# A convolution and GLU kernel: the GLU products as two 64-row tiles that change banks half way

## The chip, the cores and the metric

The kernel runs on one core of a Trainium2 chip. The metric is the device time of one execution in microseconds; two runs gave 587.36 and 587.61, median 587.49.

## The reference

A is a long convolution (S4D) over 2048 positions and 512 channels, B a bilinear GLU, and a gate per position mixes the two:

```python
g = sigmoid((x * gate_w).sum(-1, keepdims=True))
K = 2.0 * einsum("dn,dnl->dl", C, exp((A * dt)[:, :, None] * pos)).real
a = irfft(rfft(u_t, 2 * L) * rfft(K, 2 * L), 2 * L)[:, :, :L]   # transposed back, + u * D_skip
b = einsum("bsf,fd->bsd", (x @ w_gate) * (x @ w_up), w_down)    # F = 1792, D = 512
return g * a + (1 - g) * b
```

## The kernel before, in words

All GLU products are done in f32r, TensorE's rounded 32-bit form. For accuracy each operand is split into a rounded value (`hi`) and a remainder (`lo`), and each product of a 128-row block is three matmuls: lo·hi, hi·lo and hi·hi (`THREE`). The convolution (tiles named k) runs in plain float32, partly with small tiles of the array.

The GLU takes the 1792 hidden channels as 14 blocks `f` of 128, in four groups of 3, 3, 4 and 4 (`GROUPS`), and the 2048 positions in four chunks `ci` of 512. `glu()` (line 690) goes through the 16 pairs of group and chunk. For each `f` of the group, `hidden(f)` (line 596) computes gate and up: four contraction blocks `kt`, three matmuls each, into the PSUM bank `pg`, then the same into `pu`; each matmul has 128 columns of weights and 512 positions. That is 56 calls. Then a chain of four operations makes `h`: ScalarE copies `pg`, VectorE multiplies by `pu`, ScalarE rounds to `hh`, VectorE takes the remainder `hl`. Only the very first step (`f == 0` of the first chunk) goes by `kt` first and needs each part of the weights as it lands.

`down` (line 623) multiplies the group's `h` by the down weights, for the four 128-row blocks `r` of the chunk in two halves (0, 1) and (2, 3). Each block sums over the group's `f` in one bank `y`. For blocks 0 and 1 the products of the group's last `f` come last for both blocks (`late`), so that the chain to its `hl` has time. `evacuate` (line 634) scales a bank by 1 - g on ScalarE into `acc`, from where it is written or added to the output in DRAM; in the last group and chunk the sums stay on the chip, and blocks 2 and 3 are read by VectorE straight from PSUM in `ends` (line 655).

PSUM has eight banks. Line 401 gives the convolution four (`ps_k`) and the GLU four: `pg` and `pu` one each (`ps_g`) and `y` two in turn (`ps_y`).

The order of all work is set by a planner, the class `Work` (line 197). Each piece of work is a task with an engine, a duration, the tiles that it reads and writes, and a rank; `run` (line 301) lays the tasks out in time, each engine one after the other, picking what can start first and then the lower rank. `ready` (line 252) is when a task may follow another. The instructions are then issued in that order, and `InOrder` (line 116) holds every engine's order as it was laid out. So a changed task moves the order of everything after it. All instructions are issued through `InOrder`, which is why the profile shows one line, L124, for all. A GLU product is a task of 0.681 us (three matmuls).

A task may name parts of a tile, `(tile, part)`, and then waits only for work on the same part.

Of the kernel before, what the change touches and what calls it, by code (L numbers as in the profile page):

```python
# [18 lines left out]
P = 128  # L19
# [122 lines left out]
class Tile:  # L142


    def __init__(self, work, pool, tag, shape, dtype, bufs, loose):
        self.pool, self.tag, self.shape, self.dtype, self.bufs, self.loose = pool, tag, shape, dtype, bufs, loose
        self.writers, self.readers = [], []
# [13 lines left out]
        return self.ap  # L161


class Task:
    def __init__(self, n, engine, us, fn, rank, after, dma):
        self.n, self.engine, self.us, self.fn, self.rank, self.after, self.dma = n, engine, us, fn, rank, after, dma
        self.deps, self.tiles, self.start, self.end, self.rows, self.many = set(), [], None, None, (), 0


class Bus:  # L170
# [26 lines left out]
class Work:  # L197
# [8 lines left out]

    LAG = {"pe": 0.06, "sp": 0.3, "pool": 0.3}
    PE_LAG = 0.17

    OVERLAP = {"act": 0.09, "dve": 0.08}  # L210

# [89 lines left out]
    def run(self):  # L301
# [10 lines left out]
        while any(left.values()):  # L312
# [40 lines left out]
            rows.update((r, t.end) for r in t.rows)  # L353
            for tile in t.tiles:
                if tile.made is None:
                    tile.made = start
                    tile.had.append(tile)
            order.append(t)
        for t in order:
# [5 lines left out]
def gated_mix_kernel(  # L365
# [211 lines left out]

    THREE = ((1, 0), (0, 1), (0, 0))

    def product(pg, which, w, x, kt, after, first):  # L580
        base = which * D + kt * P
        part = ("k", kt) if first else which

        three = THREE[::-1] if first else THREE

        def fn():
            for n, (a, b) in enumerate(three):
# [4 lines left out]
        add("pe", 0.681, fn, r=[(w[0], part), (w[1], part), x], w=[pg], rank=2, after=after)  # L592

    steps = []

    def hidden(f):

        pg = [new("ps_g", n, [P, D]) for n in ("pg", "pu")]
        x = dict(xs)
        after = T_STEP * len(steps) - 5.0  # L600
        steps.append(f)
        pairs = [(which, kt) for which in range(2) for kt in range(KT)]
        if f == 0:

            pairs.sort(key=lambda p: p[1])
# [14 lines left out]
        )  # L620
        return hh, hl

    def down(y, r, h, w, first, last):
        def fn():
            for n, (a, b) in enumerate(THREE):
                pe.matmul(
                    y.t, h[a].t[:, r * P : (r + 1) * P], w[b].t, start=first and n == 0, stop=last and n == 2
                )

        add("pe", 0.681, fn, r=[*h, *w], w=[y], rank=2)  # L630

    ending = []

# [56 lines left out]
    def glu():  # L690
# [10 lines left out]
        for n, (gi, ci) in enumerate(order):  # L701
            fs = GROUPS[gi]
            if ci != old:
                if gi == 0 and ci <= 2:
                    ahead(ci)
                for kt in range(KT):
                    tokens(gi, ci, kt)
            old = ci
            hs = {f: hidden(f) for f in fs}
            ends = n % 4 == 3 and gi + 1 < len(GROUPS)  # L710
            if ends:
                weights(GROUPS[gi + 1])

            for rr in ((0, 1), (2, 3)):
                ys = {r: new("ps_y", "y", [P, D], bufs=2) for r in rr}
                late = fs[-1:] if rr[0] == 0 else []
                for r in rr:
                    for f in fs:
                        if f not in late:
                            down(ys[r], r, hs[f], wd[f], f == fs[0], f == fs[-1])  # L720
                    if not late:
                        evacuate(gi, ci, r, ys[r])
                if late:
                    for r in rr:
                        down(ys[r], r, hs[fs[-1]], wd[fs[-1]], False, True)
                        evacuate(gi, ci, r, ys[r])
            if ends:
                down_weights(GROUPS[gi + 1])

# [760 lines left out]
```

## Time and profile before

| | |
|---|---|
| median of two runs | 587.49 us |
| span of the profiled execution (first to last instruction) | 586.6 us |
| granted TensorE clock, mean | 1.000 |
| last matmul's start | 582.46 us |
| DMA, mean over the span | 232 GB/s |

The profiled execution's own time is 0.9 us over its span. In the profile PE is TensorE's matmuls and PEld its weight loads; DVE is VectorE, ACT ScalarE, POOL GpSimd, SP the engine that issues most DMAs. A row of the timeline has the start, the duration, the engine, the operation, the tile written and the tiles read, the array tile used (rows by columns), the shape, and how many were merged (x2); the bracket is the engine's idle time before it and what released it. Rows of groups have the total busy time and the mean of one in ns, then the idle time before them. Rows of waits have the total in us, the number and the longest. In the row of a stage each engine has its busy time and its number of instructions, in the order PE, PEld, DVE, ACT, POOL, then the granted clock, the DMA share and GB/s. A matmul's duration is modelled and covers its whole way through the array, so the next one starts before it ends.

### The profile page before, as it was taken

The numbers are of one execution on the slowest core, as the hardware profiler recorded it, in microseconds if no ns is written. First come the engines' busy times: TensorE is split into PE (matmuls) and PEld (weight loads), VectorE is DVE, ScalarE is ACT, GpSimd is POOL, SyncE is SP. The second block draws the span as 40 slices with busy tenths as digits, with TensorE's granted clock in tenths as the row PEclk, the third lists the DMA queues.
The fourth block names the chain that finished last, engine by engine and source line by source line (L and its number), as shares of the span: only waits on it lengthen the run. The fifth ranks groups of instructions, "written<-read, shape, count | busy, mean of one in ns | idle before, by whom it ended". The sixth has DMA issues, their size and how long they took to land.

```text
span 586.6 us, 14827 instructions
## 1 busy us (share of the span) xinstructions
PE 576.4 (98%) x5996; PEld 433.9 (74%) x5996; DVE 511.3 (87%) x812; ACT 399.0 (68%) x891; POOL 113.4 (19%) x159
## 2 busy tenths in 40 slices
PE   8999999999989999999999999999999999999997
PEld 5777777877876777887777778777878787677775
DVE  6998999999999999999799999995999982367664
ACT  5468888898578589876968764899696523443351
POOL 0002222311102231310412200421321104011011
PEclk9999999999999999999999999999999999999999
DMA  8999969997647698998697859899958349899976
GB/s 276 383 369 357 374 241 319 289 257 212 125 154 181 194 272 205 228 245 297 135 257 249 183 180 304 158 187 276 221 136 212 65 143 230 290 270 253 283 159 125
DMA packets 71687, 136.28 MB, mean 232 GB/s; under 512 B 6852, under 2 KB 35780, under 8 KB 69188
## 3 DMA queue, kind: packets, MB, share of 16 engines
q1 hardware_dynamic: 47668, 87.10, 43.0%
q0 software_dynamic: 23392, 47.98, 39.5%
q8 instruction: 47, 0.77, 0.6%
q10 hardware_dynamic: 560, 0.26, 0.2%
q14 instruction: 20, 0.16, 0.1%
HBM read 80.27 MB, written 55.05 MB: 231 GB/s over the span
## 4 chain that ended last, share of the span: by engine, by line
PE 83%; DVE 6%; ACT 4%; DMA 4%; issue 1%; SPq 0%; DVEq 0%; ACTq 0%
PE pg L124 23%; PE pu L124 23%; PE y L124 22%; PE k L124 16%; DVE v L124 1%; DMA pb<-par_d 1%; DMA xs_d<-xs 1%; DVE x L124 1%; DMA y<-in_xT 1%; DMA xs<-xs_d 1%; ACT acc L124 1%; DVE t L124 1%; ACT ev L124 1%; ACT xs L124 1%; ACT e L124 1%
## 5 line engine op out<-in xcount | busy, mean ns | idle before, releaser
L124 PE MATMUL pg<-xs,whi 128*128 128x512 f32 x448 | 138.9, 391 | 1.0 <-DVE xs L124 0.6
L124 PE MATMUL pu<-xs,whi 128*128 128x512 f32 x448 | 138.3, 390 | 0.0
L124 PEld LDWEIGHTS pg<-xs,whi 128*128 128x128 f32 x448 | 84.2, 188 | 20.2 <-ACT whi L124 2.0
L124 PEld LDWEIGHTS pu<-xs,whi 128*128 128x128 f32 x448 | 84.2, 188 | 16.9
L124 PE MATMUL y<-dhi,hl 128*128 128x512 f32 x224 | 90.3, 403 | 2.9 <-DVE hl L124 2.4
L124 PE MATMUL pu<-xs,wlo 128*128 128x512 f32 x224 | 90.1, 402 | 0.0
L124 PE MATMUL pg<-xs,wlo 128*128 128x512 f32 x224 | 89.4, 399 | 0.4 <-ACT h L124 0.4
L124 PE MATMUL y<-dlo,hh 128*128 128x512 f32 x224 | 87.5, 391 | 0.0
L124 PE MATMUL y<-dhi,hh 128*128 128x512 f32 x224 | 87.3, 390 | 0.0
L124 POOL DMA_DIRECT2D out<-acc x44 | 40.2, 968 | 180.4 <-ACT acc L124 173.0
L124 ACT COPY ev<-k 128x512 f32<-128x512 f32 x112 | 58.8, 596 | 14.5 <-PE k L124 14.4
L124 ACT CAST hh<-h 128x512 fp32r<-128x512 f32 x56 | 34.6, 618 | 45.7 <-DVE h L124 45.5
L124 PEld LDWEIGHTS y<-dhi,hl 128*128 128x128 f32 x224 | 42.0, 187 | 24.4 <-issue 8.1
L124 DVE TENSOR_TENSOR h<-pu,h 128x512 f32<-128x512 f32 x56 | 38.5, 688 | 23.6 <-PE pu L124 23.0
L124 PEld LDWEIGHTS pu<-xs,wlo 128*128 128x128 f32 x224 | 42.0, 187 | 20.0 <-issue 10.7
L124 ACT ACTIVATE acc<-y,ngate 128x512 f32<-128x512 f32 x62 | 41.7, 685 | 21.9 <-PE y L124 18.9
L124 PEld LDWEIGHTS pg<-xs,wlo 128*128 128x128 f32 x224 | 42.1, 188 | 18.4 <-issue 6.9
L124 ACT COPY h<-pg 128x512 f32<-128x512 f32 x56 | 32.9, 587 | 28.3 <-PE pg L124 22.0
L124 PEld LDWEIGHTS y<-dhi,hh 128*128 128x128 f32 x224 | 42.1, 188 | 9.1
L124 PEld LDWEIGHTS y<-dlo,hh 128*128 128x128 f32 x224 | 42.1, 188 | 8.2 <-DVE dlo L124 0.3
L124 DVE TENSOR_TENSOR hl<-h,hh 128x512 fp32r<-128x512 f32 x56 | 38.4, 686 | 3.0 <-ACT hh L124 2.7
L124 PEld LDWEIGHTS k<-v,x 128*32 128x32 f32 x2048 | 30.6, 109 | 6.4 <-issue 4.7
(130 smaller groups left out, 965.4 us busy)
## 6 DMA issues: line engine op xcount, KB each, us to landing
xs<-xs_d SPq DMA_DIRECT2D x36, 512.0 KB, 5.8
out<-acc POOLq DMA_DIRECT2D x44, 256.0 KB, 5.9
raw<-in_wts SPq DMA_DIRECT2D x33, 256.0 KB, 5.6
xs_d<-xs SPq DMA_DIRECT2D x16, 512.0 KB, 6.6
su_d<-ev POOLq DMA_DIRECT2D x32, 256.0 KB, 6.3
y_d<-ts SPq DMA_DIRECT2D x28, 256.0 KB, 4.9
in<-su_d POOLq DMA_DIRECT2D x12, 512.0 KB, 5.9
sk_d<-ev SPq DMA_DIRECT2D x6, 1024.0 KB, 5.4
```

The lines of the kernel that those rows point to most:

```text
L124: got = getattr(self.engine, name)(*args, **kw)
```

## The change

A new helper, `paired`, takes over all GLU products except the first gate/up step. It works for two PSUM banks at a time: `pg` and `pu` in `hidden`, or the two row blocks' `y` in `down`. Every 128-row contraction block is cut into two 64-row halves, each with its own 64-row tile of the array (`tile_position` 0 and 64). In the first half of a call tile 0 (upper rows) works for bank 0 and tile 1 (lower rows) for bank 1; then TensorE is drained, and in the second half tile 0 works for bank 1 and tile 1 for bank 0. Every bank so gets both halves of each contraction. A task is now six half matmuls for one block in one half of the call, planned at 0.647 us, the first after the drain at 0.2 more. Tasks of the second half depend on all of the first. Gate and up, and the two row blocks, are now finished at the same time, and the order with `late` in the down products is gone. The four GLU banks become one ring (`ps_g`, four buffers) from which gate, up and the down sums are all taken.

```diff
+    SWAP = 0.0
...
         if d.engine == task.engine == "pe":
-            return d.end
+            return d.end + (self.SWAP if d is task.follows else 0.0)
...
-    pools = {n: open_pool(n, b, PSUM) for n, b in (("ps_y", 2), ("ps_g", 1), ("ps_k", 4))}
+    pools = {n: open_pool(n, b, PSUM) for n, b in (("ps_g", 4), ("ps_k", 4))}
...
+    def paired(pair, products, reads, after=0.0):
+
+        n, opened, firsts = len(products), [False, False], []
+        for swap in range(2):
+            tasks = []
+            for i, (hi, lo, right) in enumerate(products):
+
+                def step(swap=swap, i=i, hi=hi, lo=lo, right=right):
+                    if swap and i == 0:
+                        pe.drain()
+                    for j, (a, b) in enumerate(THREE):
+                        for lane in range(2):
+                            k = lane ^ swap
+                            rows = slice(64 * lane, 64 * lane + 64)
+                            pe.matmul(
+                                pair[k].t, (hi, lo)[a](k, rows), right(rows, b), start=not opened[k],
+                                stop=swap == 1 and i == n - 1 and j == 2, tile_position=(64 * lane, 0),
+                            )
+                            opened[k] = True
+
+                task = add("pe", 0.647 + 0.2 * (swap and i == 0), step, r=reads[i], w=[(x, ("step", swap, i)) for x in pair], rank=2, after=after)
+                if swap:
+                    task.deps.update(firsts + tasks[:1])
+                    task.follows = firsts[-1]
+                tasks.append(task)
+            firsts = tasks
...
+    def handed():
+        x = new("ps_g", "g", [P, D], bufs=4, loose=True)
+        x.handed = True
+        return x
...
     def hidden(f):
 
-        pg = [new("ps_g", n, [P, D]) for n in ("pg", "pu")]
+        pg = [handed() for _ in range(2)]
...
-        for which, kt in pairs:
-            product(pg[which], which, ws[f], x[kt], kt, after, not steps[1:] and f == 0)
+        if not steps[1:]:
+            for kt in range(KT):
+                for which in range(2):
+                    product(pg[which], which, ws[f], x[kt], kt)
+        else:
+            w = ws[f]
+            cut = lambda n, kt: (lambda k, s: w[n].t[s, k * D + kt * P : k * D + kt * P + P])
+            paired(
+                pg, [(cut(0, kt), cut(1, kt), lambda s, b, kt=kt: x[kt].t[s, b]) for kt in range(KT)],
+                [[*((t, which) for t in w for which in range(2)), x[kt]] for kt in range(KT)], after,
+            )
...
-    def down(y, r, h, w, first, last):
...
+    def down(ys, rr, hs, fs):
+        cut = lambda t: (lambda k, s: t.t[s, rr[k] * P : rr[k] * P + P])
+        paired(
+            ys, [(cut(hs[f][0]), cut(hs[f][1]), lambda s, b, f=f: wd[f][b].t[s]) for f in fs],
+            [[*hs[f], *wd[f]] for f in fs],
+        )
...
             for rr in ((0, 1), (2, 3)):
-                ys = {r: new("ps_y", "y", [P, D], bufs=2) for r in rr}
-                late = fs[-1:] if rr[0] == 0 else []
...
+                ys = [handed() for _ in rr]
+                down(ys, rr, hs, fs)
+                for r, y in zip(rr, ys):
+                    evacuate(gi, ci, r, y)
```

More of the change, by code (lines that the diff above doesn't have):

```diff
@@ L167, in __init__ @@
         self.deps, self.tiles, self.start, self.end, self.rows, self.many = set(), [], None, None, (), 0
+        self.follows = None
 class Bus:
@@ L355, in run @@
                 if tile.made is None:
-                    tile.made = start
+                    tile.made, tile.place = start, len(tile.had)
                     tile.had.append(tile)
@@ L578, in gated_mix_kernel, with product @@
     THREE = ((1, 0), (0, 1), (0, 0))
-    def product(pg, which, w, x, kt, after, first):
+    def paired(pair, products, reads, after=0.0):
[21 more added lines that the diff above has]
+            firsts = tasks
+    def product(pg, which, w, x, kt):
         base = which * D + kt * P
-        part = ("k", kt) if first else which
-        three = THREE[::-1] if first else THREE
         def fn():
-            for n, (a, b) in enumerate(three):
+            for n, (a, b) in enumerate(THREE[::-1]):
                 pe.matmul(
@@ L590, in fn @@
                 )
-        add("pe", 0.681, fn, r=[(w[0], part), (w[1], part), x], w=[pg], rank=2, after=after)
+        add("pe", 0.681, fn, r=[(w[0], ("k", kt)), (w[1], ("k", kt)), x], w=[pg], rank=2)
+    def handed():
+        x = new("ps_g", "g", [P, D], bufs=4, loose=True)
+        x.handed = True
+        return x
     steps = []
     def hidden(f):
-        pg = [new("ps_g", n, [P, D]) for n in ("pg", "pu")]
+        pg = [handed() for _ in range(2)]
         x = dict(xs)
@@ L621, in hidden @@
         return hh, hl
-    def down(y, r, h, w, first, last):
[L624 to L630, printed above, removed]
+    def down(ys, rr, hs, fs):
[4 more added lines that the diff above has]
+        )
     ending = []
```

15 lines of the change are left out of this document (1 added, 14 removed).

## The prediction

> **What bounds the kernel now.** I read the profile's page first: busy time of the engines and the chain that ended last.
>
> ```profile
> PE 576.4 (98%) x5996; PEld 433.9 (74%) x5996; DVE 511.3 (87%) x812; ACT 399.0 (68%) x891; POOL 113.4 (19%) x159
> ...
> PE 83%; DVE 6%; ACT 4%; DMA 4%; issue 1%; SPq 0%; DVEq 0%; ACTq 0%
> PE pg L124 23%; PE pu L124 23%; PE y L124 22%; PE k L124 16%; DVE v L124 1%; DMA pb<-par_d 1%; DMA xs_d<-xs 1%; DVE x L124 1%; DMA y<-in_xT 1%; DMA xs<-xs_d 1%; ACT acc L124 1%; DVE t L124 1%; ACT ev L124 1%; ACT xs L124 1%; ACT e L124 1%
> ```
>
> TensorE (PE) is nearly always busy and carries 83% of the chain; the GLU products (pg, pu, y) are 68% of the span. So what an edit does to TensorE's time reaches the end almost whole. What TensorE waits for by name is little:
>
> ```profile
> PE y L124 <- DVE hl L124: 2.4, 2, 1.6
> ...
> PE k L124 <- issue: 0.6, 1, 0.6
> ...
> PEld k L124 <- issue: 24.5, 73, 0.8
> ...
> L124 PEld LDWEIGHTS y<-dhi,hl 128*128 128x128 f32 x224 | 42.0, 187 | 24.4 <-issue 8.1 <-DVE hl L124 4.7 <-ACT acc L124 2.5
> ```
>
> The second view is the groups of instructions, shapes kept apart, for the number of products:
>
> ```profile
> L124 PE MATMUL pg<-xs,whi 128*128 128x512 f32 x448 | 138.9, 391 | 1.0 <-DVE xs L124 0.6 <-ACT whi L124 0.5
> L124 PE MATMUL pu<-xs,whi 128*128 128x512 f32 x448 | 138.3, 390 | 0.0
> L124 PE MATMUL y<-dhi,hl 128*128 128x512 f32 x224 | 90.3, 403 | 2.9 <-DVE hl L124 2.4 <-ACT acc L124 0.2
> L124 PE MATMUL pu<-xs,wlo 128*128 128x512 f32 x224 | 90.1, 402 | 0.0
> L124 PE MATMUL pg<-xs,wlo 128*128 128x512 f32 x224 | 89.4, 399 | 0.4 <-ACT h L124 0.4
> L124 PE MATMUL y<-dlo,hh 128*128 128x512 f32 x224 | 87.5, 391 | 0.0
> L124 PE MATMUL y<-dhi,hh 128*128 128x512 f32 x224 | 87.3, 390 | 0.0
> ```
>
> That is 2016 matmuls of 128 rows by 512 columns. Their 0.39 us is a latency, overlapped by the next one; the step is read from starts in the timeline:
>
> ```profile
> 210.37 0.39 PE L124 MATMUL y<-dhi,hl 128*128 128x512 f32 x1
> ...
> 213.32 0.39 PE L124 MATMUL y<-dlo,hh 128*128 128x512 f32 x1
> 213.54 0.39 PE L124 MATMUL y<-dhi,hh 128*128 128x512 f32 x1
> ```
>
> From 210.37 to 213.54 lie 14 steps (15 starts), 3.17 / 14 = 0.2265 us each. 2016 of them are 457 us.
>
> VectorE must be kept in mind as the second engine: in the stage from 25 to 150 us it is as full as TensorE, so time won on TensorE there would be worth less.
>
> ```profile
> 25.00:150.00 125.00, 122.86 (x937) 92.33 (x938) 121.38 (x202) 102.53 (x229) 27.88 (x44) 1.00 0.92 303
> ```
>
> **The change, part by part.**
>
> **1. Two 64-row tiles side by side.** All but the first of the 56 gate/up steps and all 32 down calls are rewritten; the first step keeps its 24 full matmuls, so 2016 - 24 = 1992 matmuls become 1992 pairs of half-height ones, twice the instructions with the same 512 columns each. No pair of f32r half tiles stands in this trace. The nearest rows are the kernel transform's, four 32-row tiles with 128 columns of weights and 512 moving columns:
>
> ```profile
> L124 PEld LDWEIGHTS k<-kt,w1k_t 32*128 32x128 f32 x128 | 5.8, 184 | 6.4 <-issue 5.7 <-ACT v L124 0.4 <-ACT whi L124 0.4
> ...
> 175.62 0.61 PE L124 MATMUL pg<-xs,whi 128*128 128x512 f32 x2
> ...
> 176.17 0.31 PEld L124 LDWEIGHTS k<-kt,w1k_t 32*128 32x128 f32 x8 [0.35 <-issue]
> ...
> 176.70 0.20 PEld L124 LDWEIGHTS k<-kt,w1k_t 32*128 32x128 f32 x4 [0.22 <-issue]
> ...
> 177.13 0.20 PEld L124 LDWEIGHTS k<-kt,w1k_t 32*128 32x128 f32 x4 [0.22 <-issue]
> ```
>
> Four tiles run in one round, and rounds follow at 177.13 - 176.70 = 0.43 us. The code calls 64 of these products and the trace has 128, and one takes more than a full f32r step for the same columns, so I take a round as two streams of 512 columns (an estimate): 0.43 / 2 = 0.215 us a stream, against 0.2265 in the full array. The 0.0115 us that a full step loses beyond its stream is not lost in tiles. At that price the pairs save 1992 x 0.0115 = 22.9 us. The bounds: nothing, if each half tile keeps the step of 0.2265; 26.9 us at 0.213 (0.43 is rounded to 0.01). That the halves run one after the other is excluded by the four tiles of a round. I take 22.9, since tiles are nearer to tiles.
>
> The loads need a look too: a pair takes two loads of 128 columns. In the rows above four such loads, 0.184 us each, take 0.20 together, so loads of different rows run side by side. Against this stands the Trainium skill, page "TensorE: Matmul & The Clock Gate", section "LDWEIGHTS (loading the stationary operand)": a load's time goes by its columns and not by its rows, 128 / 1.2 = 107 ns, so half the rows would not halve it; two in a row would be 214 ns a pair, as long as the stream. The row agrees on the size of one and disagrees that they queue; taken in series the rule is rival B below.
>
> **2. The drain half way.** Each paired call ends its first half with a drain of TensorE, because a tile then writes the bank that its neighbour has just written. Calls: 55 gate/up and 32 down, 87 drains. What stands behind one is all of TensorE's queue; what waits for that is ScalarE's and VectorE's evacuation and, through them, the next pair. The trace has no drain inside the work. Its nearest rows are the last matmul and its reader, and a restart:
>
> ```profile
> 576.36 1.37 ACT L124 ACTIVATE acc<-y,ngate 128x512 f32<-128x512 f32 x2 [4.11 <-PE y L124]
> ...
> 577.10 0.19 PEld L124 LDWEIGHTS y<-dhi,hl 128*128 128x128 f32 x1 [0.52 <-ACT acc L124]
> ...
> 577.21 0.19 PEld L124 LDWEIGHTS y<-dlo,hh 128*128 128x128 f32 x1
> ...
> 580.16 0.75 DVE L124 SCALAR_TENSOR_TENSOR kt<-y,ngate,kt 128x512 f32<-128x512 f32 x1 [1.70 <-PE y L124]
> ...
> 582.46 0.39 PE L124 MATMUL y<-dhi,hh 128*128 128x512 f32 x1
> 582.88 0.88 DVE L124 SCALAR_TENSOR_TENSOR kt<-y,ngate,kt 128x256 f32<-128x256 f32 x2 [1.97 <-PE y L124]
> ```
>
> A matmul is seen as done 582.88 - 582.46 = 0.42 us after its start. After a restart the first matmul streams 0.11 us after its load (577.10 to 577.21, where the next load marks its start). Without a drain the next pair would come 0.215 after the last. So a drain costs 0.42 + 0.11 - 0.215 = 0.315 us, 87 of them 27.4 us. Lower bound: a change of tile shape. The second matmul of the row at 175.62 starts at 175.85 and the loads of another shape at 176.17, 0.32 later: 0.32 + 0.11 - 0.215 = 0.215, in all 18.7 us. Upper bound: the wake-up besides. The first acc of the row at 576.36 ends near 577.05 (half of 1.37), the load follows at 577.10; with 0.05 more, 0.365 and 31.8 us. I take 0.315: the drain is there for finished writes, which the reader waits for too.
>
> The Trainium skill, page "PSUM — Partial Sum Buffer", section "PSUM bank collisions raise a hardware error", says that different row tiles may not write the same bank at one time and that software has to see to it; no run here shows it. By it the drain can't be left out, and the 27.4 us are the price of two tiles sharing two banks.
>
> **3. Both halves end together.** Before, the gate bank was done one stretch of 12 matmuls ahead of the up bank and its copy ran beside them. Now copy, product, cast and remainder stand in a row behind the pair:
>
> ```profile
> L124 ACT COPY h<-pg x56: 560/589/617, 11.3 to 566.4; 128x512 f32<-128x512 f32 x56
> L124 DVE TENSOR_TENSOR h<-pu,h x56: 678/691/693, 12.2 to 570.4; 128x512 f32<-128x512 f32 x56
> L124 ACT CAST hh<-h x56: 601/621/652, 12.9 to 571.1; 128x512 fp32r<-128x512 f32 x56
> L124 DVE TENSOR_TENSOR hl<-h,hh x56: 662/684/711, 14.0 to 572.1; 128x512 fp32r<-128x512 f32 x56
> ```
>
> 0.2 (0.42 less the step) + 0.59 + 0.69 + 0.62 + 0.68 = 2.8 us from the last pair to the remainder that the down call needs. The cover of the last step of a chunk shrinks: before, two row blocks' products for the other f (4 or 6 products of 0.68, 2.7 or 4.1 us); now the first half of the paired call without the last f (2 or 3 steps of 0.645, 1.3 or 1.9). Uncovered: 1.5 us in eight chunks, 0.9 in eight, 19 us, from which one step of the next gate/up product in each chunk (its first token tile is there early) takes 16 x 0.645 = 10.3. At most some 9 us stay, less where convolution work fits in. I take 3.
>
> **4. One ring of four banks.** A down call no longer waits for its own two banks; the group row above shows 2.5 us lost to ACT acc, mostly beside other work. I take 1 gained, between 0 and 2.5.
>
> **5. Start and end.** A pair needs gate and up weights, so the second step starts when the second remainder is done, 10.93 + 1.29 = 12.22 and a hand-over, against 11.91: 0.4 us.
>
> ```profile
> 10.93 1.29 DVE L124 TENSOR_TENSOR wlo<-ev,whi 128x512 fp32r<-128x512 f32 x2
> ...
> 11.91 0.50 PE L124 MATMUL pg<-xs,wlo 128*128 128x512 f32 x1
> ```
>
> At the end the last two row blocks finish together, so the sum of 0.75 us at 580.16 moves behind the last matmul, ahead of the two halves: 0.7 us. No DMA is added; the order of the others shifts with the plan, which I cost at nothing, as the chain gives DMA 4%.
>
> **Sum.** The profiled execution has a span of 586.6 us and 587.5 as its time with what lies around it (0.9); that is also the median of the runs. 587.5 - 22.9 + 27.4 + 3 - 1 + 0.4 + 0.7 = 595.1 us.
>
> **The rivals.**
>
> A. The half tiles gain nothing: each keeps 0.2265, because what the full array loses belongs to the load and swap of f32r weights, not to the array's being whole. For it: no f32r tile is in the trace, and a longer stream hides more. Against it: the rounds of 0.43. Then 595.1 + 22.9 = 618.0 us, slower. It decides from a step of about 0.217 on, where 599.2 is passed.
>
> B. Loads in series: two of 0.11 us (577.10 to 577.21), a pair each 0.22. Saved: 1992 x 0.0065 = 12.9; 605.1 us. Against it: four loads in 0.20.
>
> C. The drain costs what a change of shape does, 0.215: 595.1 - 8.7 = 586.4 us, no change. For it: that too empties the array. Against it: the added wait is for writes, not for the array.
>
> D. The drain is nearly free, 0.1 us or less, since loads go ahead of it or the plan puts other work at the swap: 595.1 - 87 x 0.215 = 576.4 us or below, to 568. For it: 73 idle spells of the loads before k show how often other work already breaks the products.
>
> E. The longer chain to the remainder is not covered (9 us instead of 3), and the 32 down calls, which now need two free banks at once, wait 0.2 each for the second: 595.1 + 6 + 6.4 = 607.5 us. Against it: TensorE's waits on hl are 2.4 us now.
>
> **How the numbers follow.** Forecast 595.1, chance 0.35, by its own bounds 589 to 601. A 0.14, B 0.08, C 0.22, D 0.14, E 0.07. Two per cent, about what a measurement of this kernel can tell from no change, is 575.7 to 599.2. Faster: most of D, 0.12. Slower: A, B, most of E and the forecast's upper edge, 0.14 + 0.08 + 0.06 + 0.04 = 0.32. Within: 0.56. The range has to reach into D and most of A: 574 to 614; below lies some 0.09, above some 0.08.
>
> **What would show it.** Starts of the half matmuls of one lane 0.215 apart (0.2265: A; 0.22: B). A gap of 0.53 us between the last start before a drain and the first stream after it (0.43: C; below 0.32: D). TensorE's waits for hl near 3 us in place of 2.4 in all (over 9: E). Last matmul to end 0.7 us longer. Forecast wrong if the time leaves 589 to 601, even if two errors hide each other in the total.

## The result, and the profile after

The changed kernel took 645.88 and 649.05 us, median 647.46, against 587.49: a ratio of 1.1019 (95% interval 1.0954 to 1.1084), 60.0 us slower. The forecast was 595.1, the range ended at 614. The profiled execution took 649.05 with a span of 647.3. Its clock was 0.991 in the mean, against 1.000 before.

From the profile's page, busy times and the chain that ended last; then, with shapes kept apart, the largest group of products:

```profile
PE 612.7 (95%) x7988; PEld 445.7 (69%) x7988; DVE 514.5 (79%) x812; ACT 399.8 (62%) x891; POOL 113.5 (18%) x159
...
PE 79%; DVE 9%; DMA 6%; issue 3%; ACT 3%; SPq 0%; DVEq 0%; ACTq 0%
PE g L124 65%; PE k L124 14%; DVE v L124 2%; DMA raw<-in_wts 2%; DMA kt<-in_wts 1%; DVE y L124 1%; DVE h L124 1%; DVE hl L124 1%; DMA in<-in_wts 1%; DVE x L124 1%; ACT h L124 1%; DMA ev<-in_wts 1%; DVE ri L124 1%; DMA pb<-par_d 1%; DVE m L124 0%
```

```profile
L124 PE MATMUL g<-xs,whi 64*128 64x512 f32 x1760 | 279.0, 389 | 0.3 <-issue 0.3
```

The other engines' busy times are as before within 3.2 us, so the same other work ran over a longer span. TensorE's busy time rose by 36.3 us, its idle time from 10.2 us (586.6 - 576.4) to 34.6 (647.3 - 612.7). VectorE's share of the chain rose from 6% to 9%. The groups have 1760 half matmuls with whi where 896 full ones were (448 for gate, 448 for up); 16 of these, of the first step, stayed full, and the other 880 were doubled. So the change did what it says.

The timeline of TensorE in a calm stretch gives the step of a pair:

```profile
118.07 0.39 PE L124 MATMUL g<-xs,wlo 64*128 64x512 f32 x2
118.30 0.62 PE L124 MATMUL g<-xs,whi 64*128 64x512 f32 x4
118.75 0.40 PE L124 MATMUL g<-xs,wlo 64*128 64x512 f32 x2
...
121.47 0.40 PE L124 MATMUL g<-xs,wlo 64*128 64x512 f32 x2
```

From 118.07 to 121.47 lie 15 pairs: 3.40 / 15 = 0.2267 us a pair, the step of a full matmul before. Nothing was gained; this is the reading that the prediction had named for rival A. The timeline around a drain:

```profile
305.57 0.61 PE L124 MATMUL g<-xs,whi 64*128 64x512 f32 x4
306.27 0.50 PE L124 MATMUL g<-xs,wlo 64*128 64x512 f32 x2
306.37 0.42 PEld L124 LDWEIGHTS g<-xs,whi 64*128 64x128 f32 x4
306.60 0.63 PE L124 MATMUL g<-xs,whi 64*128 64x512 f32 x4
```

Between 305.57 and 306.60 are three steps, two pairs in the first row and one after the drain: 1.03 us instead of 3 x 0.2265 = 0.68. The drain cost 0.35. In the table of busy times it shows in part only, since a matmul counts as busy for 0.39: the engine is idle from 306.19 (305.80, the start of the second pair of the row at 305.57, + 0.39) to 306.27, 0.08 us a drain and 7 us in all, and the rest of the drain is counted as busy. After it the first step is still long (306.27 to 306.60, 0.33), since the load of its own weights lies open there: it starts with the matmul's row at 306.27, and the next load 0.10 later, at 306.37.

TensorE's waits, and the first row of VectorE's (its waits before began with DVE h <- PE pu, 23.0 us):

```profile
PE k L124 <- DVE y L124: 6.5, 1, 6.5
PE g L124 <- ACT h L124: 3.9, 5, 2.2
PE g L124 <- issue: 3.2, 6, 1.7
PE k L124 <- issue: 1.9, 3, 0.8
PE g L124 <- DVE h L124: 1.8, 3, 0.8
PE g L124 <- DVE hl L124: 1.6, 4, 0.6
```

```profile
DVE h L124 <- ACT h L124: 43.2, 30, 4.4
```

VectorE's product now waits for ScalarE's copy, not for the up bank: the copy is on the path. But TensorE waits for hl 1.6 us only. These rows name 18.9 of TensorE's 34.6 us of idle time and the drains another 7; the rest is in smaller groups.

Two of these holes had a sequel. The table by stages of after (the last figures are the granted clock, the DMA share and GB/s), with the timeline of one:

```profile
126.40:130.00 3.60, 1.15 (x7) 0.45 (x5) 1.54 (x4) 2.93 (x6) 0.00 (x0) 1.00 0.33 110
130.00:133.40 3.40, 3.40 (x17) 2.36 (x15) 3.30 (x7) 3.40 (x17) 0.86 (x1) 0.50 0.52 69
...
478.20:485.00 6.80, 3.17 (x56) 2.50 (x58) 6.73 (x14) 2.62 (x7) 0.85 (x1) 0.50 0.39 65
```

```profile
126.37 0.41 PE L124 MATMUL g<-dhi,hh 64*128 64x512 f32 x2
127.07 0.62 ACT L124 CAST whi<-raw 128x512 fp32r<-128x512 f32 x1 [2.39 <-DMA raw<-in_wts]
...
128.33 0.56 ACT L124 COPY h<-g 128x512 f32<-128x512 f32 x1
...
128.95 0.50 PE L124 MATMUL g<-dhi,hl 64*128 64x512 f32 x1 [2.17 <-ACT h L124]
...
130.12 1.04 PE L124 MATMUL g<-dhi,hh 64*128 64x512 f32 x2
130.54 1.04 PE L124 MATMUL g<-dhi,hl 64*128 64x512 f32 x2
```

After a wait of 2.17 us for ScalarE's copy of a gate bank, TensorE ran 3.4 us at half its clock, pairs 0.42 apart. The copy itself came late: ScalarE, which works in its planned order, had stood 2.39 us before it at the landing of a DMA of weights (raw). The wait of 6.5 us for y ended within another such stretch, in which TensorE was busy for 3.17 us. Half of the busy time, (3.40 + 3.17) / 2 = 3.3 us, is lost to that and no wait lists it. Before had a clock of 1.000.

### The profile page after: what moved, and what is told of

The parts are those of the page before. It is cut to its first block, busy times and chain, and to the rows that moved or that the text cites. A ratio compares the mean times of both kernels' runs of the same rounds, so it can differ in the third digit from the quotient of the medians.

```text
span 647.3 us, 18837 instructions
## 1 busy us (share of the span) xinstructions
PE 612.7 (95%) x7988; PEld 445.7 (69%) x7988; DVE 514.5 (79%) x812; ACT 399.8 (62%) x891; POOL 113.5 (18%) x159
## 3 DMA queue, kind: packets, MB, share of 16 engines
q8 instruction: 63, 1.03, 0.6%
## 4 chain that ended last, share of the span: by engine, by line
PE 79%; DVE 9%; DMA 6%; issue 3%; ACT 3%; SPq 0%; DVEq 0%; ACTq 0%
PE g L124 65%; PE k L124 14%; DVE v L124 2%; DMA raw<-in_wts 2%; DMA kt<-in_wts 1%; DVE y L124 1%; DVE h L124 1%; DVE hl L124 1%; DMA in<-in_wts 1%; DVE x L124 1%; ACT h L124 1%; DMA ev<-in_wts 1%; DVE ri L124 1%; DMA pb<-par_d 1%; DVE m L124 0%
## 5 line engine op out<-in xcount | busy, mean ns | idle before, releaser
L124 PE MATMUL g<-xs,whi 64*128 64x512 f32 (+1 forms) x1776 | 284.6, 389 | 0.5 <-issue 0.3
L124 PE MATMUL g<-xs,wlo 64*128 64x512 f32 (+1 forms) x888 | 192.8, 412 | 8.4 <-issue 1.9
L124 PEld LDWEIGHTS g<-xs,whi 64*128 64x128 f32 (+1 forms) x1776 | 177.6, 185 | 30.0 <-ACT whi L124 1.8
L124 PEld LDWEIGHTS g<-xs,wlo 64*128 64x128 f32 (+1 forms) x888 | 89.8, 184 | 66.6 <-issue 49.3
L124 PE MATMUL g<-dhi,hl 64*128 64x512 f32 x448 | 100.7, 420 | 9.7 <-ACT h L124 2.5
L124 PE MATMUL g<-dlo,hh 64*128 64x512 f32 x448 | 94.2, 392 | 0.0
L124 PE MATMUL g<-dhi,hh 64*128 64x512 f32 x448 | 94.0, 391 | 0.0
L124 PEld LDWEIGHTS g<-dhi,hl 64*128 64x128 f32 x448 | 46.8, 185 | 43.8 <-issue 24.8
L124 PEld LDWEIGHTS g<-dhi,hh 64*128 64x128 f32 x448 | 47.0, 186 | 7.9
L124 PEld LDWEIGHTS g<-dlo,hh 64*128 64x128 f32 x448 | 46.3, 186 | 5.3
```

The source lines that it names most:

```text
L124: got = getattr(self.engine, name)(*args, **kw)
```

## The experiments

The theory at this point: half tiles are worth nothing in f32r (A), the drains cost about 0.35, and the remaining 25 to 30 us come from the new order. The rivals: the half tiles are slower than they look, or the planner was misled by its planned costs, or the drains cost far more by what they delay. Each kernel below has the median of four runs and its ratio to seven of the kernel before on the same chip (their medians were 587.8 to 588.9), except the two kernels of single steps, which ran once. Differences between two kernels are those of their medians.

### What half tiles and types cost: steps

A kernel of its own: 24 rounds of matmuls for each form, one form after the other.

```python
section("full", 1, 128)            # f32r, also with 384 and 256 moving columns, 64 weight columns
section("pair", 2, 64)             # two 64-row tiles, two banks
section("quad", 4, 32)
section("one64", 1, 64)            # one lane alone
section("fp32", 1, 128, dtype=F32);  section("fp32pair", 2, 64, dtype=F32)
section("bf16", 1, 128, dtype=BF16); section("bf16pair", 2, 64, dtype=BF16)
section("drain", 2, 64, drain=6)   # a drain and a swap every 6 pairs
```

> A kernel of its own, not the mixture: 24 matmuls (or rounds of tiles) of each of 13 forms back to back, to read the step of each form from the trace. Theory 'added swap': the 0.0135 us that a full f32r matmul takes beyond its stream of 512 columns is added at every change of weights, so 256 columns step in about 0.107 + 0.0135 = 0.12 us, 384 in 0.174, a 64-row pair and a 32-row round in 0.2265, float32 in 0.427 + 0.0135. Rival 'load chain': a matmul can't start until about 0.2265 us after the one before, because its load starts with that one and takes so long; then 384 and 256 columns step in 0.2265 too, pairs in 0.2265, and float32 in 0.427 with nothing added. Rival 'tiles are free of it' (the prediction's): pair and round 0.215. A drain between two rounds: 0.34 us more than a step, as in the trace of after.

Timeline rows from inside each section (start, length of the merged row, how many):

```profile
25.70 4.50 PE L41 MATMUL b<-x,w_pair 64*128 64x512 f32 x38
...
36.84 3.34 PE L41 MATMUL b<-x,w_one 64*128 64x512 f32 x14
...
45.53 14.76 PE L41 MATMUL b<-raw,w_fp 128*128 128x512 f32 x34
...
66.76 13.47 PE L41 MATMUL b<-raw,w_fp32pair 64*128 64x512 f32 x62
...
86.83 3.40 PE L41 MATMUL b<-xb,w_bf 128*128 128x512 bf16 x15
...
91.68 3.62 PE L41 MATMUL b<-xb,w_bf16pair 64*128 64x512 bf16 x32
```

A step is the row's length less one matmul's latency, over the steps in it. f32r pairs: (4.50 - 0.39) / 18 = 0.228; one lane alone: (3.34 - 0.39) / 13 = 0.227. bf16: (3.40 - 0.38) / 14 = 0.216 full and (3.62 - 0.38) / 15 = 0.216 in pairs. Plain float32 runs as two instructions a product (48 for 24), and each steps at (14.76 - 0.59) / 33 = 0.429 full and (13.47 - 0.59) / 30 = 0.429 in pairs; taken as two streams, as the prediction took a round, that is 0.2147 a stream. So the type decides, not the tile: f32r takes about 0.2265 and bf16 0.216 in the full array and in tiles alike, and float32 has the prediction's 0.43 in the full array too. The groups of the shorter f32r streams:

```profile
L41 PE MATMUL b<-x,w_full 128*128 128x384 f32 x24 | 4.3, 335 | 0.0
...
L41 PE MATMUL b<-x,w_full 128*128 128x256 f32 x24 | 3.0, 282 | 0.0
```

(4.3 - 0.335) / 23 = 0.172 and (3.0 - 0.282) / 23 = 0.118: 0.054 for every 128 columns, of which four make 0.216. So about 0.01 us of an f32r step doesn't go with the columns.

### Is it the change of weights: steps2

```python
section("again", 1, 128)               # f32r, new weights each time
section("same", 1, 128, step=0)        # f32r, the same weights each time
section("m128", 1, 128, moving=128);   section("c32", 1, 128, cols=32)
section("quad256", 4, 32, moving=256)
section("fulldrain", 1, 128, drain=6); section("pairdrain", 2, 64, drain=6)
section("b16", 1, 128, dtype=BF16);    section("b16drain", 1, 128, dtype=BF16, drain=6)
```

> A second kernel of its own for the 0.0135 us that every f32r matmul took beyond its stream, in full array, pairs and rounds alike, and that float32 and bf16 did not take. Theory 'change of weights': it is paid for exchanging the weights, so the same weights 24 times over step in 0.2155 and 32 columns of weights in less than 0.2265. Rival 'every f32r matmul': the same weights and 32 columns step in 0.2265 too, 128 moving columns in 0.053 + 0.0135 = 0.067, and a 32-row round of 256 columns in 0.12. A drain every 6: 0.35 us more than a step in the full array as in pairs, if its price is the emptying of the array and not the tiles' change of bank.

Timeline rows of the products, and then of the loads in the sections with drains:

```profile
13.15 5.60 PE L41 MATMUL b<-x,w_again 128*128 128x512 f32 x24
18.59 5.60 PE L41 MATMUL b<-x,w_same 128*128 128x512 f32 x24
24.03 2.79 PE L41 MATMUL b<-x,w_m 128*128 128x128 f32 x24
26.66 5.72 PE L41 MATMUL b<-x,w_c 128*32 128x512 f32 x24
32.31 3.14 PE L41 MATMUL b<-x,w_quad 32*128 32x256 f32 x96
```

```profile
37.12 1.23 PEld L41 LDWEIGHTS b<-x,w_fulldrain 128*128 128x128 f32 x6 [0.51 <-issue]
38.84 1.22 PEld L41 LDWEIGHTS b<-x,w_fulldrain 128*128 128x128 f32 x6 [0.50 <-issue]
...
45.63 1.23 PEld L41 LDWEIGHTS b<-x,w_pairdrain 64*128 64x128 f32 x12 [0.51 <-issue]
47.36 1.23 PEld L41 LDWEIGHTS b<-x,w_pairdrain 64*128 64x128 f32 x12 [0.50 <-issue]
...
55.69 0.98 PEld L41 LDWEIGHTS <-w_b16drain 128*128 128x128 bf16 x6 [0.57 <-issue]
57.24 0.98 PEld L41 LDWEIGHTS <-w_b16drain 128*128 128x128 bf16 x6 [0.57 <-issue]
```

New and repeated weights both give (5.60 - 0.389) / 23 = 0.2266, and weights of 32 columns, whose load is shorter (0.108 us in the median against 0.188), (5.72 - 0.394) / 23 = 0.232. So neither the exchange of the weights nor the length of their load makes the addition, against "the load and swap of f32r weights", the cause that rival A had named. A fixed price of every f32r load isn't excluded, since each of these products came with a load of its own (24 and 24). The Trainium skill, page "TensorE: Matmul & The Clock Gate", section "Back-to-back issue gap", gives N / 2.4 + 2.5 ns for a matmul by itself. At 512 columns that is 215.8 (an estimate): the trace agrees for bf16 (216) and not for f32r (226.6). The 128-column product missed its expectation of 0.067: (2.79 - 0.27) / 23 = 0.110, about as long as a load takes (0.11, from 577.10 to 577.21 in the prediction's rows). Rounds of four 32-row tiles with 256 columns, (3.14 - 0.28) / 23 = 0.124, have four such loads in one step: loads of different rows run side by side, and rival B falls. A drain adds 38.84 - 37.12 - 6 x 0.2265 = 0.36 to full matmuls, 0.37 to pairs, 57.24 - 55.69 - 6 x 0.216 = 0.25 to bf16.

### The drains alone: before_drains, rows_drains

The kernel before with 87 drains, at the places nearest to the change's:

```diff
# product, before
+            if not first and which == 1 and kt == 0:
+                pe.drain()
# down, before
+            if first and r % 2:
+                pe.drain()
```

> The kernel before with the 87 drains alone, at the middle of each gate/up step and of each down call, no tiles and nothing else changed. If a drain costs what the trace of after shows at it (0.343 us): 587.5 + 29.8 = 617 us. Rival 'drains upset the order': all that after lost beyond is their work too, 630 to 647 us. The prediction's price of 0.315: 615 us.

618.65 us, 1.052 (1.0502 to 1.0537): 30.6 more than before, 0.352 a drain, the micro kernel's price. So drains delay little beyond themselves. The same in the change's order, with full matmuls (full_rows, next):

```diff
+                    if swap and i == 0:
+                        pe.drain()
```

> full_rows with the 87 drains, planned at 0.681 and 0.343 us: the changed kernel in all but the half tiles. If the price of order (24.7 us) and of drains (30.6) simply add and half tiles cost and gain nothing: 588.5 + 55.3 = 643 to 647 us. If drains fall partly into waits that the order has anyway: 630 us. If half tiles cost something of their own, it is what the changed kernel's 647.5 has over this.

645.38 us, 1.0988 (1.0949 to 1.1027): 32.6 over full_rows, 0.375 a drain. This kernel is the change with full matmuls in place of pairs, apart from the place of a down call's last `f` (see full_rows), and the two differ by 2.1 us with intervals that overlap (1.0954 to 1.1084). So the half tiles gain nothing, and here they cost nothing that can be told.

### The order alone: full_rows, no_swap

The change's tasks, order and ring, with full 128-row matmuls that alternate between the two banks, and no drain. One thing is not as in the change: a task is now one product for one bank, so in a down call the last `f` comes behind the other `f` of both blocks, as with `late`. In the change it is needed at the end of the first half already. The shorter cover that the prediction worked out is therefore not in this kernel, nor in those below that keep its down calls.

```diff
-                    if swap and i == 0:
-                        pe.drain()
+                    m, k = divmod(n * swap + i, 2)
+                    hi, lo, right = products[m]
...
-                        for lane in range(2):
...
-                task = add("pe", 0.647 + 0.2 * (swap and i == 0), step, r=reads[i], w=[(x, ("step", swap, i)) for x in pair], rank=2, after=after)
+                task = add("pe", 0.681, step, r=reads[(n * swap + i) // 2], w=[(x, ("step", swap, i)) for x in pair], rank=2, after=after)
```

> The changed kernel's order (both banks of a call side by side and finished together, ring of four banks, no late block) with full 128-row matmuls, planned at 0.681 us a task; no half tiles, no drains. If the new order itself costs the 30 us that drains don't explain: 617 us. If they come from a plan that counts tiles and drains too short: 588 to 592 us. The prediction's parts 3 to 5 by themselves, with E not true: 587.5 + 3 - 1 + 0.4 + 0.7 = 590.6 us.

612.74 us, 1.0424 (1.0406 to 1.0441): 24.7 over before with the same 5996 matmuls. This is the finding that the prediction had least room for. Its page, first stage and waits:

```profile
PE 587.0 (97%) x5996; PEld 439.5 (72%) x5996; DVE 513.4 (84%) x812; ACT 397.4 (65%) x891; POOL 113.4 (19%) x159
```

```profile
25.00:150.00 125.00, 119.97 (x821) 88.95 (x820) 120.92 (x203) 99.77 (x225) 25.28 (x41) 0.99 0.88 285
```

```profile
PE k L124 <- DVE kt L124: 6.3, 2, 3.3
PE k L124 <- ACT hh L124: 2.8, 1, 2.8
PE k L124 <- ACT ev L124: 2.0, 3, 0.7
```

TensorE is idle 20.6 us (607.6, its span, - 587.0) against 10.2, and its busy time is 10.6 longer, (3.40 + 5.37) / 2 = 4.4 of it from two stretches at half clock:

```profile
44.20:47.60 3.40, 3.40 (x15) 1.50 (x5) 3.37 (x8) 3.02 (x13) 2.33 (x4) 0.50 0.96 343
324.10:330.90 6.80, 5.37 (x36) 3.07 (x37) 6.80 (x9) 4.58 (x7) 1.81 (x2) 0.50 0.22 42
```

This execution, 609.56 us, is the fastest of the four. Its mean clock was 0.991, that of the others 0.983, 0.978 and 0.978. From 2 x (1 - clock) x span one can estimate 11 us at half clock in this one and 21 to 27 in the others, of which at most half is lost; so in the median the stretches can weigh up to 12 us. Between 25 and 150 us TensorE does 821 matmuls where it did 937. The named waits are those of the convolution (k) for VectorE and ScalarE.

The other single edit to the change: each lane keeps its bank, so no drain is needed.

```diff
-                    if swap and i == 0:
-                        pe.drain()
...
-                            k = lane ^ swap
+                            k = lane
...
-                task = add("pe", 0.647 + 0.2 * (swap and i == 0), step, r=reads[i], w=[(x, ("step", swap, i)) for x in pair], rank=2, after=after)
+                task = add("pe", 0.647, step, r=reads[i], w=[(x, ("step", swap, i)) for x in pair], rank=2, after=after)
```

> The changed kernel with its half tiles, but each tile stays with its bank, so there is no drain and the 0.2 in the plan is gone; each bank so gets one half of the contraction twice and the other not at all. If the half tiles gain nothing and the drains are 30 of the 60 us: 617 us. If the waits after the drains are theirs too: near 590 to 595. If tiles gained 0.0115 us a pair after all: 570 us.

621.86 us, 1.0581 (1.0544 to 1.0617). It is 25.6 under after, and 9.1 over full_rows, where none was due if half tiles are free and all else is alike. The clock doesn't explain the 9.1: the four runs had 0.981, 0.989, 0.989 and 0.988, most of them above full_rows. But all else is not alike: no_swap needs the last `f` of a down call in its first half, as the change does, and plans a task at 0.647. So half tiles and the earlier need of hl together cost 2.1 us with drains (after against rows_drains) and 9.1 without; the runs don't divide this between them.

### Is the planner misled: true_costs

```diff
-                task = add("pe", 0.647 + 0.2 * (swap and i == 0), step, r=reads[i], w=[(x, ("step", swap, i)) for x in pair], rank=2, after=after)
+                task = add("pe", 0.681 + 0.343 * (swap and i == 0), step, r=reads[i], w=[(x, ("step", swap, i)) for x in pair], rank=2, after=after)
```

> The changed kernel with nothing but the planner's durations set to what was measured: 0.681 us a task in place of 0.647 and 0.343 in place of 0.2 at the drain. If the 5 us that order (24.7) and drains (30.6) leave of the 60 come from a plan that is too short: 588 + 24.7 + 30.6 = 643 us. If a wrong plan costs more than that and some of the other two is its work: 620 to 635 us. If it costs nothing: 647 us.

649.12 us, 1.101 (1.0983 to 1.1036), as after. The planned costs aren't the cause.

### Which part of the order: one_by_one, gate_up_alone, down_alone, own_banks, no_late

Each is full_rows with one thing put back; no_late is the kernel before with one thing taken. In one_by_one both kinds of call finish one bank before the other (the tiles that a task reads and the bank that it writes are named to match, here and in the next two):

```diff
-                    m, k = divmod(n * swap + i, 2)
+                    m, k = i, swap
```

> As full_rows (full 128-row matmuls, ring of four banks, no late block), but one bank of a call after the other: gate then up, row block then row block, each bank taken and released by itself. If the 24.7 us of full_rows come from both banks ending together: 588 to 592 us. If they come from the shared ring of four or from the late block's going: 608 to 613 us.

596.65 us, 1.0129 (1.0083 to 1.0175), between the two forecasts. In gate_up_alone this holds for gate and up only, in down_alone for the down calls only:

```diff
-                    m, k = divmod(n * swap + i, 2)
+                    m, k = (i, swap) if alone else divmod(n * swap + i, 2)
```

> As full_rows, but gate and up one after the other; the down calls keep their two banks side by side. full_rows was 612.7 us, both kinds one after the other 596.7. If gate and up ending together make the 16 us between them (the longer chain to the remainder): 597 us. If the down calls ending together make them: 612 us.

> As full_rows, but the two row blocks of a down call one after the other; gate and up side by side. If gate and up ending together make the 16 us: 612 us. If the down calls do: 597 us.

592.28 us, 1.0067 (1.0041 to 1.0092), and 606.64 us, 1.0323 (1.0293 to 1.0353). So putting gate and up back in a row gains 20.4 us, putting the down blocks back 6.1. In gate_up_alone TensorE is as full as before:

```profile
PE 578.5 (98%) x5996; PEld 435.2 (74%) x5996; DVE 511.6 (87%) x812; ACT 398.9 (68%) x891; POOL 113.3 (19%) x159
```

own_banks gives full_rows the PSUM banks of before:

```diff
-    pools = {n: open_pool(n, b, PSUM) for n, b in (("ps_g", 4), ("ps_k", 4))}
+    pools = {n: open_pool(n, b, PSUM) for n, b in (("ps_y", 2), ("ps_g", 1), ("ps_k", 4))}
...
-        pg = [handed() for _ in range(2)]
+        pg = [new("ps_g", n, [P, D]) for n in ("pg", "pu")]
...
-                ys = [handed() for _ in rr]
+                ys = [new("ps_y", "y", [P, D], bufs=2) for _ in rr]
```

> As full_rows (both banks side by side, ended together, no late block), but with the banks of before: gate and up one each, the down sums two in turn. If the 24.7 us come from the shared ring: 588 to 592 us. If from ending together: 612 us or more, since gate and up of the next step now wait for VectorE's product of this one with no second pair.

621.04 us, 1.0538 (1.0516 to 1.0561): the ring makes the new order 8 us cheaper. Without it TensorE waits for the readers of gate's bank and of up's (5.1 us for DVE h), where full_rows waits 0.3 us for them:

```profile
PE pg L124 <- ACT h L124: 8.4, 8, 4.1
```

no_late takes the late block out of the kernel before:

```diff
-                late = fs[-1:] if rr[0] == 0 else []
+                late = []
```

> The kernel before without its late block: a chunk's first two row blocks sum straight through. If the 8 us that remain with banks one after the other (596.7 against 588.9) come from the late block's going: 596 us. If from the ring: 588 us.

593.0 us, 1.0087 (1.0064 to 1.0109), 5.2 more. one_by_one lacks `late` too and lies 7.8 over before. Paired down calls, which put the last f last for both blocks again, win 4.4 of that back (gate_up_alone).

### Why gate and up together cost 20 us: late_copy, alone_late_copy, gate_ahead, copy_aside

The theory: the copy (0.59 us) moves behind the last product. The rival: it is the pair of banks being taken and filled at once. First the copy alone is made late, in before (late_copy) and in gate_up_alone (alone_late_copy), with the same edit:

```diff
-        add("act", 0.59, lambda: act.copy(h.t, pg[0].t), r=[pg[0]], w=[h], rank=0)
+        add("act", 0.59, lambda: act.copy(h.t, pg[0].t), r=pg, w=[h], rank=0)
```

> The kernel before with one word changed: ScalarE's copy of the gate bank also waits for the up bank, so the chain to the remainder gets longer by the copy, 0.59 us, and nothing else differs (banks, order of the products, late block, full matmuls, no drains). If the 20.4 us that gate and up ending together cost (612.7 against 592.3) are the longer chain alone: 605 to 608 us. If the shared ring and the pair's two banks at once are needed for it: 588 to 593 us.

> gate_up_alone (gate then up, each bank by itself, ring of four; 592.3 us) with the copy waiting for both banks, as in late_copy, but with the ring, so that the next step needn't wait for this copy. If the chain makes the 20.4 us: 605 to 613 us. If late_copy's 13.8 were the wait for its single gate bank and the chain costs little: 592 to 596 us.

late_copy: 602.14 us, 1.0222 (1.0192 to 1.0253), 13.8 more, most of it in the first row of TensorE's waits, for the single gate bank:

```profile
PE pg L124 <- ACT h L124: 10.4, 13, 2.3
```

alone_late_copy, where the ring takes that wait away: 600.98 us, 1.0218 (1.0183 to 1.0254), 8.7 over gate_up_alone. Now the reverse, in full_rows. gate_ahead lets a bank's readers start when that bank is done; copy_aside takes the copy off the chain (it copies the bank onto itself, and the product takes a weight tile instead of h):

```diff
# gate_ahead
-                task = add("pe", 0.681, step, r=reads[(n * swap + i) // 2], w=[(x, ("step", swap, i)) for x in pair], rank=2, after=after)
+                task = add("pe", 0.681, step, r=reads[(n * swap + i) // 2], w=[pair[(n * swap + i) % 2]], hold=pair, rank=2, after=after)
# copy_aside
-        add("act", 0.59, lambda: act.copy(h.t, pg[0].t), r=[pg[0]], w=[h], rank=0)
+        add("act", 0.59, lambda: act.copy(pg[0].t, pg[0].t), w=[pg[0]], rank=0)
...
-            "dve", 0.69, lambda: dve.tensor_tensor(out=h.t, in0=pg[1].t, in1=h.t, op=ALU.mult),
-            r=[pg[1], h], w=[h], rank=0,
+            "dve", 0.69, lambda: dve.tensor_tensor(out=h.t, in0=pg[1].t, in1=ws[f][0].t[:, :D].bitcast(F32), op=ALU.mult),
+            r=[pg[1], (ws[f][0], 0)], w=[h], rank=0,
```

> full_rows with the banks named one by one: gate and up still side by side and taken as a pair, but gate's last task ends one task (0.68 us) ahead of up's and is known to, so the copy of 0.59 us runs beside up's last matmuls. If the longer chain is the cause of the 20.4 us: 592 to 598 us. If it is that both banks are taken and filled at once: 608 to 613 us.

> full_rows with the copy taken out of the chain: ScalarE still copies the gate bank (onto itself, in PSUM), and VectorE's product takes the up bank and a weight tile that is there already, so the gate's values are left out of h. Banks, pairs, order and all other work as in full_rows (612.7 us). If the chain, longer by the copy, makes the 20.4 us that gate and up ending together cost: 592 to 598 us. If two banks taken and filled at once make them: 608 to 613 us.

603.23 us, 1.0257 (1.0219 to 1.0295), and 601.22 us, 1.0231 (1.02 to 1.0261): 9.5 and 11.5 us under full_rows. Each of the four fell between its two forecasts, so neither theory holds by itself. The chain itself, worked out from the traces as the mean over the 56 steps of the time from the start of a step's last gate or up matmul to the end of its hl: 3.39 us before, 4.09 in full_rows, 4.10 in after, 3.61 in copy_aside, but 4.06 in gate_ahead. So a copy that waits for both banks costs 8.7 us in one order, and a copy off the chain gives 11.5 back in the other: 9 to 12 of the 20 us, by two edits from opposite sides. That the length of the chain is the reason isn't shown. gate_ahead gained about as much with a mean chain as long and with the pair still taken at once, so another order of the plan may be worth as much by itself. Nor does the mean chain rank the kernels: it is 4.62 in down_alone (606.6 us) and 4.56 in alone_late_copy (601.0), both faster than full_rows with 4.09. The remaining 9 to 12 us stay open too.

## Why the prediction was wrong

The sum as measured, by kernels that add one thing each: order and ring +24.7 (full_rows), drains +32.6 (rows_drains), half tiles with the earlier need of hl +2.1 (after), together 59.4 of the 60.0. Forecast were +3.1 for order, ring, start and end (3 - 1 + 0.4 + 0.7), +27.4 and -22.9.

**Part 1, the half tiles: the step that failed is "I take 22.9, since tiles are nearer to tiles".** Pairs step at 0.2267. The row taken as nearest, the rounds of 0.43 of the kernel transform, differed from the products in two things, tile and type, and the working noted only the tile. Its operands are plain float32, which the 128 instructions for 64 products betrayed, and a float32 instruction steps at 0.429 in the full array as well (steps). So 0.215 was the type's price, and 22.9 us were never there. Rival A forecast this step rightly; of its cause, load and swap, the runs exclude the exchange of weights and the length of the load (steps2), and its price on its own, 618.0, was too low by the order. In the look at the loads, "The row agrees on the size of one" misreads the row, which has 0.184 us a load; a load that lay open took 0.11 (577.10 to 577.21).

**Part 2, the drain: right, a little small.** 0.315 was forecast, 0.35 measured in after, in the micro kernels and as 30.6 / 87. The gap from the last start to the first stream, forecast 0.53, is 306.27 + 0.10 - 305.80 = 0.57, with 0.10 from the load that lies open (306.27 to 306.37). C and D fall. The term is 30.6 to 32.6 instead of 27.4.

**Part 3, both halves end together: the term was mis-sized, 3 instead of more than 20, since it left out what gate and up side by side cost in every step.** The working counted the cover of one place only, the last step of each of the 16 chunks, and bounded it by 9. The runs put 20.4 us on gate and up ending together (full_rows against gate_up_alone), where the mean chain of the 56 steps became 0.7 us longer. In the kernel before, gate was done 2.7 us or more ahead of up in 52 of them, as its trace shows; `f == 0` of all four chunks, and not the very first step alone, went by `kt` with gate 0.68 us ahead. The shorter cover that the working did price is not in these 20.4 us, since full_rows keeps the old one. Its 3 us were not far off: no_late against before, and one_by_one against gate_up_alone, shorten the cover with gate and up in a row, and cost 5.2 and 4.4. With gate and up side by side it didn't show as a loss: down_alone has the shorter cover and is 6.1 under full_rows. In after its price lies with that of the half tiles in the 2.1 us over rows_drains. Rival E had the direction, but its mark was wrong: TensorE's waits for hl fell from 2.4 to 1.6. The loss shows as waits of the convolution for VectorE and ScalarE, as stretches at half clock (4.4 us in the fastest run of full_rows, by their clocks more in the others), and in smaller gaps. That the lengthened chain pushes the convolution's work to worse places would fit this, but it was argued, not shown, and gate_ahead speaks against the chain as the only reason.

**Part 4, the ring: right in sign, by another way.** It is worth 8 us in the new order rather than 1, because without it TensorE waits for the readers of gate's and up's banks, 8.4 and 5.1 us, and only 0.3 for acc, the wait that the working named (own_banks). With one bank after the other no gain shows: one_by_one, with the ring, lies 7.8 over before, no_late, without it, 5.2, and their intervals overlap. So that the sign came out was luck.

**Part 5:** the stretch behind the last matmul was to grow by 0.7. The last rows of after give

```profile
642.25 0.40 PE L124 MATMUL g<-dhi,hh 64*128 64x512 f32 x2
642.69 1.53 DVE L124 SCALAR_TENSOR_TENSOR kt<-g,ngate,kt 128x512 f32<-128x512 f32 x3 [2.45 <-PE g L124]
```

647.3 - 642.25 = 5.05 us from the last matmul to the end, 4.1 before (586.6 - 582.46): 0.9 more. The start's 0.4 is too small for these runs to tell. The shifted order of the DMAs was put at nothing; in after one wait, the 2.17 us at 128.95, goes back to a DMA of weights, with 3.4 us at half clock behind it. The planned costs, which the working left out, matter little (true_costs).

**The range** moved one term at a time: A ended at 618, E at 607.5, and no case held both. A and E together, 595.1 + 22.9 + 12.4 = 630.4, would have been short still: the order's 24.7 lay outside every bound that was given for it.

## What to carry to other kernels

When a price comes from the nearest row of a trace, list every way in which that row differs, the data type first, and test the same difference on a row that shares the type. Splitting a full contraction into row tiles gains nothing where a full array streams as fast, and each change of banks behind a drain costs its 0.35 us. When two results that finished one after the other are made to finish together, look at every step and not only at the last of a chunk; the order can be tried by itself, with nothing else of the change, if each task still waits for the same things at the same place.

## What the runs showed of the hardware

- An f32r matmul of 512 columns, each with its load, takes a step of 0.2265 us in the full array, in 64-row pairs (0.228 in steps) and in a single lane (0.227), with new or repeated weights; bf16 takes 0.216 in the full array and in pairs. A float32 product is two instructions of 0.429 each, in both.
- A drain costs 0.35 to 0.37 us among f32r matmuls, full or in pairs, and 0.25 among bf16, where the first step after it is 0.22 long (steps2) against 0.33 in f32r.
- With waits of TensorE of 2.2, 3.3 and 6.5 us (after, full_rows, after) came stretches of 3.4, 6.8 and 6.8 us at a clock of 0.50, the latter two beginning within the wait. The Trainium skill, page "TensorE: Matmul & The Clock Gate", section "What's actually happening", has the clock fall to half after an idle window of about 3.4 us that runs freely. The lengths agree, one window and two; but the wait of 2.2 us, with 0.3 more soon after it, was shorter than such a window, and the stretch of 3.4 us at 44.20 in full_rows came after waits of only 0.66 and 0.74 us.
